# Two MLP weights decoded in a stream of their own ahead of their use, their loads on the GpSimd queue, and a later scan instruction in a complex linear attention kernel

## The chip, the cores and the metric

The kernel runs on one core of one Trainium2 chip. The time is device microseconds of one execution. Three runs of the kernel before gave 1078.79, 1084.68 and 1078.61 us, median 1078.79. Engines are named as in the profile: PE is TensorE, DVE VectorE, ACT ScalarE, POOL GpSimd, SP SyncE.

## The reference

Three stages follow each other. The attention is a linear recurrence over 768 time steps for 4 batches and 8 heads of width 48, with a complex decay per channel:

```
mag   = sqrt(a_re^2 + a_im^2);  scale = min(mag, 0.999) / (mag + 1e-6)
S_re, S_im = a_re*scale * S_re - a_im*scale * S_im + k (x) v,  a_re*scale * S_im + a_im*scale * S_re
y[t]  = q[t] . S_re
```

The 3072 tokens with their 384 channels then go through a gated MLP, `x = ((x @ w1) * (x @ w2)) @ w3 @ w_out` with a hidden width of 1024, and through a second MLP, `h = x @ w_in` of width 2048, `g = h * tanh(softplus(h))`, `out = g @ w_out2`. Everything is float32 outside the chip.

## The kernel before

**Attention.** The 768 steps of a batch are cut into chunks of 128 tokens, 24 in all. Inside a chunk the recurrence becomes matmuls on keys and queries that are scaled with running products of the decays. These products are made by `bh_stream(g)` for three groups of eight chunks; all eight chunks of a group, with both halves of each, lie side by side on 128 partitions, so that a group is 65 steps long. A group goes in blocks of 7 steps (10 blocks: nine of 7 and one of 2). For each block `norm` computes the limited decays on VectorE and ScalarE (its last results are the planes of `an`, lines 240 and 241, and the squares `rv`, line 246), `inverse` runs one scan instruction on VectorE over `rv` (line 270) for the reciprocals, `steps` does the recurrence of the products with two dependent VectorE instructions a step (lines 292 and 293), and `scaled` multiplies keys and queries by both into the tile `kt` (lines 310 and 313), which POOL's queue stores to the DRAM buffer `kq_d` with three DMAs (lines 315 and 317). `table` closes a group with six small instructions (lines 327 to 332) that need the `fs` copies of lines 299 to 302.

`ch_stream` then works chunk by chunk: it loads a chunk's keys `tm` from `kq_d` with two DMAs on SP (line 390), transposes them on TensorE (`ps_tr`, line 421), forms the chunk's contribution to the state (`ps_u`), the scores (`ps_a`, masked into `am` on VectorE) and the outputs (`ps_y`), and stores them to DRAM. Four chunks make an x tile of 512 tokens, six in all; it is loaded back as `xl` (line 496) and split into a high and a low part.

**First MLP.** Before everything else `fold_stream` multiplies w3 by w_out on TensorE. `m1_stream(i)` then takes x tile i through w1 and w2 (`pa`, `pb`) and through the folded matrix (`acc`), in eight column blocks j. Every product is three matmuls of high and low parts (`mm3`, line 549). The weights arrive as 64-bit values. `decode` loads a column block into one of two buffers `raw64` on SP's queue (line 142), and turns it into float32 with two ScalarE instructions (lines 149, 160) and two VectorE instructions (lines 161, 164); `split` then writes the high part on ScalarE (line 133) and the low part on VectorE (line 134). For w1 and w2 that is `w12(j)`, called by `m1_stream(0)` just before block j is used: 16 tiles in all, 384 KB each. The split parts take the room of the fold's buffers. The second MLP (`ps_h`, `ps_o`) follows when the first is through.

**Order.** `_merge` interleaves the streams while the program is traced: each stream yields the cost of what it just traced, and the stream with the smallest sum of cost over weight goes next. A planner then orders each engine's instructions by this order and by estimated durations; an instruction that is ready may go ahead of earlier ones that are not. On the chip each engine and each DMA queue takes its instructions in that fixed order. The merges are

```
_merge((F, 24.0), (bh_stream(0), 106.0))
_merge((until(CH, 8), 59.0), (bh_stream(1), 106.0), (take(M, 90.0), 90.0))
_merge((until(CH, 16), 59.0), (bh_stream(2), 106.0), (take(M, 90.0), 90.0))
```

with F the fold, CH the chunks and M the first MLP. Blocks of `kt` have one buffer: a block's `kt` can be written when the stores of the one before have read it.

## Time and profile before

| what | value |
|---|---|
| median of 3 runs | 1078.79 us |
| the profiled execution: span | 1079.1 us |
| PE busy | 935.3 us (87%) |
| DVE busy | 702.2 us (65%) |
| ACT busy | 691.0 us (64%) |
| POOL busy | 108.9 us (10%) |
| mean granted clock of PE | 0.944 |

The span runs from the first to the last instruction; of the profiled execution it is the only time there is. A busy share over the whole span mixes stages: the fold and the first group's scan, then chunks, scans and the first MLP side by side, then the second MLP. The rows further down are therefore taken stage by stage. A row of a timeline gives start, duration, engine, line and operation, and in brackets how long the engine was idle just before and what ended that. Instructions of one engine are pipelined, so that two which follow each other can overlap by some hundredths of a microsecond.

### The profile page before, as it was taken

What the parts mean: (1) busy time and instruction counts of PE and PEld (TensorE: products, weight loads), DVE (VectorE), ACT (ScalarE), POOL (GpSimd) and SP (SyncE); (2) the same over time, 40 slices, a digit from 0 to 9 for tenths busy, and PEclk for the clock granted to TensorE, in tenths of its full rate; (3) what the DMA queues carried; (4) which work ended last, traced back from release to release, by engine and by line L of the source; (5) the groups of instructions that cost most, each with busy time, mean ns of one, the idle gap of its engine ahead of it and who ended that gap; (6) DMA issues with size and microseconds to landing.
All of it is one profiled execution on the core that took longest, in us unless ns stands there. A gap on an engine that the chain in (4) does not pass through costs nothing.

```text
span 1079.1 us, 13826 instructions
## 1 busy us (share of the span) xinstructions
PE 935.3 (87%) x4952; PEld 754.5 (70%) x4952; DVE 702.2 (65%) x1334; ACT 691.0 (64%) x1263; POOL 108.9 (10%) x161
## 2 busy tenths in 40 slices
PE   0586006879999999999999999999999999999997
PEld 0243005758788778888888888888888888887876
DVE  5989797899898999462335522688565644645552
ACT  6987466877787686574445422998656665466672
POOL 1212242222212222000000000000000000000000
PEclk9988556889999999999999999999999999999999
DMA  8675559995786875664533300122100101000000
GB/s 304 218 242 149 155 149 249 225 248 131 199 226 163 208 219 115 160 189 115 128 64 127 87 30 29 59 89 59 59 1 10 50 1 59 1 19 10 1 30 33
DMA packets 72509, 124.36 MB, mean 115 GB/s; under 512 B 7574, under 2 KB 45776, under 8 KB 71024
## 3 DMA queue, kind: packets, MB, share of 16 engines
q1 hardware_dynamic: 60880, 85.41, 28.4%
q0 software_dynamic: 11552, 37.98, 13.5%
q8 instruction: 41, 0.67, 0.3%
q14 instruction: 36, 0.29, 0.1%
HBM read 84.16 MB, written 36.18 MB: 112 GB/s over the span
## 4 chain that ended last, share of the span: by engine, by line
PE 62%; DVE 7%; DMA 3%; ACT 2%; issue 1%; SPq 0%; DVEq 0%; ACTq 0%
PE ps_h L549 18%; PE ps_o L549 17%; PE acc L549 7%; PE pa L549 7%; PE pb L549 6%; PE ps_a L464 2%; PE ps_tr L421 2%; DMA ws<-w 1%; PE ps_u L429 1%; PE ps_y L477 1%; PE ps_y L482 1%; DVE t L292 1%; DVE kt L313 1%; DVE p L293 1%; DMA out<-osb 1%
## 5 line engine op out<-in xcount | busy, mean ns | idle before, releaser
L549 PE MATMUL ps_o<-gh,wuh 128*128 128x512 f32 x288 | 113.4, 395 | 2.0 <-ACT osb L722 1.7
L549 PE MATMUL ps_o<-gl,wuh 128*128 128x512 f32 x288 | 113.3, 393 | 0.4 <-DVE gl L134 0.4
L549 PE MATMUL ps_h<-x2h,wil 128*128 128x512 f32 x288 | 113.4, 394 | 0.0
L549 PE MATMUL ps_h<-x2h,wih 128*128 128x512 f32 x288 | 113.2, 393 | 0.0
L549 PE MATMUL ps_o<-gh,wul 128*128 128x512 f32 x288 | 112.8, 392 | 0.0
L549 PE MATMUL ps_h<-x2l,wih 128*128 128x512 f32 x288 | 112.1, 389 | 0.0
L134 DVE TENSOR_TENSOR gl<-hb,gh 128x1024 fp32r<-128x1024 f32 x48 | 58.6, 1223 | 76.2 <-ACT gh L133 76.2
L692 ACT ACTIVATE wb<-ps_h 128x512 f32<-128x512 f32 x96 | 56.1, 598 | 67.9 <-PE ps_h L549 67.7
L693 DVE COPY hb<-ps_h 128x512 f32<-128x512 f32 x96 | 64.7, 687 | 49.1 <-ACT wb L692 47.2
L571 DVE TENSOR_TENSOR u<-u,pb 128x512 f32<-128x512 f32 x48 | 32.8, 684 | 69.5 <-PE pb L549 69.3
L421 PE MATMUL ps_tr<-id_sb,tm 128*96 128x128 f32 x384 | 55.6, 288 | 25.1 <-DMA tm<-kq_d 22.5
L133 ACT CAST gh<-hb 128x1024 fp32r<-128x1024 f32 x48 | 50.2, 1048 | 35.0 <-PE ps_o L549 35.0
L421 PEld LDWEIGHTS ps_tr<-id_sb,tm 128*96 128x96 f32 x384 | 44.5, 132 | 35.5 <-issue 24.3
L292 DVE TENSOR_TENSOR t<-an,p 128x192 f32<-128x192 f32 x192 | 67.4, 351 | 0.7
L133 ACT CAST uh<-u 128x512 fp32r<-128x512 f32 x48 | 29.7, 618 | 59.6 <-DVE u L571 59.4
L180 PE MATMUL ps_f<-fw1h,fw1l 128*128 128x384 f32 x48 | 24.8, 692 | 48.7 <-DVE fw1l L164 48.7
L549 PEld LDWEIGHTS ps_o<-gh,wuh 128*128 128x128 f32 x288 | 54.0, 188 | 16.8 <-ACT osb L722 4.2
L549 PEld LDWEIGHTS ps_o<-gl,wuh 128*128 128x128 f32 x288 | 54.1, 188 | 12.7 <-DVE gl L134 1.1
L549 PEld LDWEIGHTS ps_h<-x2l,wih 128*128 128x128 f32 x288 | 54.1, 188 | 12.5
L549 PEld LDWEIGHTS ps_h<-x2h,wil 128*128 128x128 f32 x288 | 54.0, 188 | 12.5
L549 PEld LDWEIGHTS ps_o<-gh,wul 128*128 128x128 f32 x288 | 54.2, 188 | 12.0
L549 PEld LDWEIGHTS ps_h<-x2h,wih 128*128 128x128 f32 x288 | 54.1, 188 | 11.3
(177 smaller groups left out, 2402.3 us busy)
## 6 DMA issues: line engine op xcount, KB each, us to landing
tm<-kq_d SPq DMA_DIRECT2D x48, 384.0 KB, 5.9
an<-in_a POOLq DMA_DIRECT2D x27, 336.0 KB, 5.0
kqt<-in_kq POOLq DMA_DIRECT2D x27, 336.0 KB, 6.6
kq_d<-kt POOLq DMA_DIRECT2D x27, 336.0 KB, 3.9
kq_d<-kt POOLq DMA_DIRECT2D x54, 168.0 KB, 5.2
vv<-in_v SPq DMA_DIRECT2D x24, 256.0 KB, 2.8
raw<-in_w SPq DMA_DIRECT2D x16, 384.0 KB, 5.5
raw<-in_win SPq DMA_DIRECT2D x16, 384.0 KB, 4.2
```

Of the source, the lines that this page charges most:

```text
L133: A.copy(out=hi, in_=raw)
L134: V.tensor_tensor(out=lo, in0=raw, in1=hi.bitcast(F32), op=sub)
L180: T.matmul(ps, lhsT=f[:, kk], rhs=wos[:, kk], start=(kk == 0), stop=(kk == 7))
L292: V.tensor_tensor(out=t, in0=win2, in1=_bc(pv[:, ::-1], 2, 2), op=mul)
L293: V.tensor_tensor(out=p[:, j], in0=t[:, 0], in1=t[:, 1], op=add)
L313: V.tensor_tensor(out=kt, in0=_bc(kqt, 3, 2), in1=_bc(p[:, 0:m], 2, 2), op=mul)
L421: T.transpose(ps[:, hh], tm[n][:, h0 + hh, z], id_sb[0:C, 0:C])
L464: T.matmul(ps[:, hh], lhsT=kf[n][:, h], rhs=qf[n][:, h], start=True, stop=True)
L549: T.matmul(ps, lhsT=l, rhs=r, start=first and n == 0, stop=final and n == len(seq) - 1)
L571: V.tensor_tensor(out=u, in0=u, in1=pb, op=mul)
L692: A.activation(out=wb[:, f % GRP], in_=ps, func=AF.Sigmoid, scale=-1.0)
L693: V.tensor_copy(hb[:, f % 2], ps)
```

## The change

The w1 and w2 tiles get a stream of their own, `w12_stream`, merged with the second stage at weight 36. Their loads go out on POOL's queue, each ordered behind a store marked in `st["pin"]`: the last `kt` store that POOL was given up to that point of the trace. `m1_stream` draws the stream on if a block is not there yet. In `bh_stream` the scan instruction is traced after the fourth step of a block (the last one where a block is shorter) and no longer ahead of its steps. `kt` gets two buffers, and the stores of the last two blocks of group 0 go to SP's queue. To make room, `x1` takes a slot of the tag `t`, and `rz` is no longer padded to a full block.

```diff
-    def decode(src, n, dst=None, raw=None, pool=None, cap=False, signs=False):
+    def decode(src, n, dst=None, raw=None, pool=None, cap=False, signs=False, queue=None):
...
-        nc.sync.dma_start(out=raw.rearrange("p n z -> p (n z)"), in_=src.bitcast(I32))
+        (queue or nc.sync).dma_start(out=raw.rearrange("p n z -> p (n z)"), in_=src.bitcast(I32))
...
-                kt = bh.tile([128, m, 2, 2, D], F32, tag="kt", name="kt", bufs=1, padded_shape=[128, BLK, 2, 2, D])
+                kt = bh.tile([128, m, 2, 2, D], F32, tag="kt", name="kt", padded_shape=[128, BLK, 2, 2, D])
...
-                nc.gpsimd.dma_start(out=kq_d[g][0:64, s0:s0 + m], in_=kt[0:64].rearrange("p s z r d -> p s (z r d)"))
+                q = nc.sync if g == 0 and i >= NB - 2 else nc.gpsimd
+                q.dma_start(out=kq_d[g][0:64, s0:s0 + m], in_=kt[0:64].rearrange("p s z r d -> p s (z r d)"))
                 for z in range(2):
-                    nc.gpsimd.dma_start(
+                    w = q.dma_start(
...
+                if q is nc.gpsimd:
+                    st["pin"] = w
...
-            x1 = bh.tile([64, 2, 2, D], F32, tag="x1", name="x1", bufs=1)
+            x1 = bh.tile([128, 2, 2, D], F32, tag="t", name="x1")[0:64]
...
-            inverse(i)
-            yield .9
             for k, w in enumerate(steps(i)):
                 yield w
+                if k == min(3, blocks[i][1] - blocks[i][0] - 1):
+                    inverse(i)
+                    yield .9
...
-    def w12(j):
-        for src, n in ((w1, "w1"), (w2, "w2")):
-            f = decode(src[:, j], 3 * 128)
-            split(f, wt[n + "h"][:, j].rearrange("p k n -> p (k n)"), wt[n + "l"][:, j].rearrange("p k n -> p (k n)"))
+    w12_done = [0]
+
+    def w12_stream():
+        for j in range(8):
+            for src, n in ((w1, "w1"), (w2, "w2")):
+                with tc.issue_after(st["pin"].ins):
+                    f = decode(src[:, j], 3 * 128, queue=nc.gpsimd)
+                split(f, *[wt[n + z][:, j].rearrange("p k n -> p (k n)") for z in "hl"])
+            w12_done[0] = j + 1
+            yield 2.0
...
-            if i == 0:
-                w12(j)
+            while w12_done[0] <= j:
+                next(W12)
...
+    W12 = w12_stream()
     _merge((F, 24.0), (bh_stream(0), 106.0))
-    _merge((until(CH, 8), 59.0), (bh_stream(1), 106.0), (take(M, 90.0), 90.0))
+    _merge((until(CH, 8), 59.0), (bh_stream(1), 106.0), (take(M, 90.0), 90.0), (W12, 36.0))
```

## Rows read from the trace of the kernel before

**Rows 1.** Busy us by stage: PE, PEld, DVE, ACT, POOL; clock, DMA, GB/s.
```profile
171.00:226.50 55.50, 45.80 (x376) 40.60 (x376) 49.03 (x116) 46.23 (x121) 13.70 (x20) 0.80 0.95 237
277.00:300.00 23.00, 21.35 (x125) 17.29 (x124) 18.95 (x50) 18.48 (x47) 5.71 (x10) 0.93 0.80 210
...
410.00:671.00 261.00, 261.00 (x1617) 218.37 (x1616) 113.43 (x203) 120.75 (x272) 7.38 (x12) 1.00 0.39 101
```

**Rows 2.** Timeline of PE, 80 to 300 us: start, duration, idle before.
```profile
151.75 0.45 PE L401 MATMUL ps_mt<-id_sb,mt 64*96 64x64 f32 x2 [46.49 <-DVE mt L330]
171.13 2.77 PE L421 MATMUL ps_tr<-id_sb,tm 128*96 128x128 f32 x12 [18.93 <-DMA tm<-kq_d]
...
226.54 0.50 PE L549 MATMUL pa<-xh,w1h 128*128 128x512 f32 x1 [2.19 <-ACT xh L133]
```

**Rows 3.** Chain of waits, 226 to 300 us: start, us, what.
```profile
277.61 5.59 DMA raw<-in_w
```

**Rows 4.** Groups of instructions, 103 to 152 us: busy, mean ns, idle before.
```profile
L161 DVE SCALAR_TENSOR_TENSOR raw<-raw 128x384 int32<-128x384 int32 x5 | 2.8, 555 | 2.8 <-ACT raw L160 2.8
L164 DVE SCALAR_TENSOR_TENSOR dec<-dec,raw 128x384 int32<-128x384 int32 x5 | 2.8, 553 | 0.0
L149 ACT ACTIVATE dec<-raw 128x384 f32<-128x384 f32 x5 | 2.7, 545 | 10.5 <-DMA raw<-in_w 10.5
...
L134 DVE TENSOR_TENSOR w1l<-dec,w1h 128x384 fp32r<-128x384 f32 x3 | 1.7, 554 | 0.0
...
L134 DVE TENSOR_TENSOR w2l<-dec,w2h 128x384 fp32r<-128x384 f32 x2 | 1.1, 556 | 0.0
```

**Rows 5.** Timeline of DVE, 120 to 230 us.
```profile
120.75 0.96 DVE L270 TENSOR_TENSOR_SCAN rs<-rv,sc 128x384 f32<-128x384 f32 x1 [3.06 <-ACT rv L246]
...
133.81 0.56 DVE L161 SCALAR_TENSOR_TENSOR raw<-raw 128x384 int32<-128x384 int32 x1 [2.75 <-ACT raw L160]
...
144.74 0.51 DVE L238 SCALAR_TENSOR_TENSOR m<-y,m 128x336 f32<-128x336 f32 x1 [1.41 <-ACT m L234]
...
146.79 1.55 DVE L313 TENSOR_TENSOR kt<-kqt,p 128x1344 f32<-128x1344 f32 x1
...
150.99 0.20 DVE L327 TENSOR_TENSOR x<-p,fs 64x96 f32<-64x96 f32 x1
...
157.34 0.35 DVE L313 TENSOR_TENSOR kt<-kqt,p 128x192 f32<-128x192 f32 x1
...
173.65 0.35 DVE L292 TENSOR_TENSOR t<-an,p 128x192 f32<-128x192 f32 x1
...
174.74 0.36 DVE L292 TENSOR_TENSOR t<-an,p 128x192 f32<-128x192 f32 x1
...
175.43 0.36 DVE L292 TENSOR_TENSOR t<-an,p 128x192 f32<-128x192 f32 x1
```

**Rows 6.** Timeline of POOL, its stores of `kt`.
```profile
137.44 1.48 POOL L317 DMA_DIRECT2D kq_d<-kt  x2
...
148.64 0.59 POOL L315 DMA_DIRECT2D kq_d<-kt  x1 [0.30 <-DVE t L292]
...
158.56 1.08 POOL L317 DMA_DIRECT2D kq_d<-kt  x2
...
165.14 1.48 POOL L317 DMA_DIRECT2D kq_d<-kt  x2
...
194.57 1.47 POOL L317 DMA_DIRECT2D kq_d<-kt  x2
```

**Rows 7.** DMA issues, 160 to 230 us: size, median us to landing.
```profile
raw<-in_w SPq DMA_DIRECT2D x3, 384.0 KB, 6.1
```

**Rows 8.** Waits of DVE, 0 to 155 us: total, times, longest.
```profile
DVE rs L270 <- ACT rv L246: 8.1, 4, 3.1
```

**Rows 9.** Timeline of SP's queue: the keys of chunks 0 and 1.
```profile
162.14 2.86 SPq L390 DMA_DIRECT2D tm<-kq_d  x4
```

**Rows 10.** Waits of SP's queue, 145 to 175 us: total, times, longest.
```profile
SPq L142 <- DVE dec L164: 23.9, 3, 13.2
```

More of the change, by code (lines that the diff above doesn't have):

```diff
@@ L186, in fold_stream @@
             wt[n] = wpo.tile([128, 8, 3, 128], F32R, tag=n, name=n)
-    tabs = {}
+    tabs, st = {}, {}
     def bh_stream(g):
@@ L194, in bh_stream @@
         blocks = [(s0, min(s0 + BLK, L + 1)) for s0 in range(0, L + 1, BLK)]
-        ans, kqs, dec, sqs = {}, {}, {}, {}
+        ans, kqs, dec, rvs, sqs = {}, {}, {}, {}, {}
         run = {}
@@ L251, in norm @@
                 V.memset(rv[0:64, :, 1], 1.0)
-            dec[i] = (an, rv)
+            dec[i], rvs[i] = an, rv
             yield .5
@@ L258, in inverse @@
             n = s1 - s0
-            rv = dec[i][1]
+            rv = rvs.pop(i)
             add1 = sc1
@@ L266, in inverse @@
             if n < BLK:
-                add1 = bh.tile([128, D * (n + 1)], F32, tag="rz", name="rz", bufs=1, padded_shape=[128, D * (BLK + 1)]).rearrange("p (d s) -> p d s", d=D)
+                add1 = bh.tile([128, D * (n + 1)], F32, tag="rz", name="rz", bufs=1).rearrange("p (d s) -> p d s", d=D)
                 V.memset(add1, 0.0)
@@ L279, in steps @@
             n = s1 - s0
-            an, _ = dec.pop(i)
+            an = dec.pop(i)
             p = run["b"] = bh.tile([128, n, 2, D], F32, tag="p", name="p", padded_shape=[128, BLK, 2, D])
@@ L367 @@
     chunks_done = [0]
-    st = {}
     zs = [ch.tile([D2, H, DP], F32, name=f"z{z}", bufs=1) for z in range(2)]
```

## The prediction

> **What bounds the kernel now.** I read the busy time by stage first, then TensorE's timeline, then what its late starts wait for. From 410 us to the MLP's second half at 671 us TensorE is busy for all of 261 us at full clock, and the scans are no longer in its way [rows 1]. Work that is always available sets the end there, so the change can only pay by letting TensorE begin its continuous work earlier. That work begins late: after the fold TensorE sits idle for 46.5 us until the first table, then 18.9 us for the keys of chunk 0, and the first matmul on x (`pa`) starts at 226.54 us [rows 2]. Between chunk 0 and that matmul it is busy 45.8 of 55.5 us, at 0.80 of its clock [rows 1]. After it there is always an x tile or a chunk to work on, with one exception: a late w load stands in the chain of waits for 5.59 us [rows 3], and 277 to 300 us shows 21.35 busy of 23 at a clock of 0.93 [rows 1]. So the forecast is a sum over four points: the end of group 0's scan, the load of chunk 0's keys, the first `pa`, and 277 to 300 us.
>
> **Scan of group 0, the decodes leave it.** Five decodes lie beside its last third though nobody needs them yet: 5 + 5 + 3 + 2 = 15 VectorE instructions, and ScalarE waits 10.5 us for their loads [rows 4]. ScalarE works in order, so these waits reach the scan: VectorE stands 3.06, 2.75 and 1.41 us, 7.2 in sum, each time for something ScalarE writes [rows 5]. An instruction placed between two steps costs less than its 0.55 us: with a decode between them two steps start 1.09 us apart (173.65 to 174.74), without it 0.69 (174.74 to 175.43) [rows 5], so 0.40 each and 15 x 0.40 = 6.0. Removal of all is worth 13.2 us. Not all goes: the first three pairs of loads are ordered behind the third write of block 7, issued at 138.9 us before [rows 6], some 10 us earlier now; with a landing of 6.1 us [rows 7] about one tile is decoded before the scan ends, 3 x 0.40 + 7.2 / 5 = 2.6 us back. **-10.6 us**, bounds -13.2 and -5 (waits as long as before, behind other loads).
>
> **Scan instruction mid-block.** VectorE waits 8.1 us in four places for `rv` ahead of line 270 up to 155 us, 3.06 of it counted above [rows 8]; 5.0 are left. But ScalarE writes the planes that the next step multiplies (lines 240, 241) right beside `rv` (line 246), so most of this wait passes on to line 292. I take -1, bounds -5 and 0.
>
> **Keys of the last two blocks.** Block 8's `kt` is written at 146.79, its store is issued at 148.64 behind the `fs` copies, block 9's `kt` (0.35 us of work) comes only at 157.34 because the one buffer is still being read, its store ends issue at 159.64, and the load of chunk 0 is issued at 162.14 [rows 5, 6, 9]. The last step is done at 150.99 [rows 5]: 11.1 us from there to the load. Sync's queue is another holder: it waited 23.9 us in three places for raw buffers, 13.2 at the longest, ahead of that load [rows 10]; the w loads leave this queue too. After: scan, product and `kt` of block 9, about 1.0 us by their widths; three stores on sync at the 0.7 us that a key load takes there (2.86 / 4) [rows 9], 2.1; a landing of at most 162.14 - 159.64 = 2.5; together 5.6. Block 8's stores end no later: 148.3 + 2.1 + 6.1 = 156.5, against 150.99 + 5.6 = 156.6. **-5.5 us**, bounds -8 and -2. POOL loses six stores. Nothing else stands behind sync's new ones but this load, which must wait for them anyway. Chunk 0's load then goes out at 162.1 - 17.1 = 145 us; its 9.0 us to 171.13 [rows 2, 9] I leave as they are (3 either way). The second `kt` buffer costs nothing later; the shared `x1` and smaller `rz` are nothing (six instructions a group).
>
> **Chunks 0 to 3, the decodes arrive.** The order mark moves on with each POOL store of `bh_stream(1)`. By the yields (10.5 of 106 a block, 2 of 36 a pair) pairs 0 to 2 stand behind block 7 of group 0, 3 and 4 behind block 0, 5 to 7 behind blocks 1 and 2 of group 1; block 2's store was issued at 194.57 [rows 6], and now some 10 us earlier. So about ten tiles, 30 instructions, 12 us, are decoded beside chunks 0 to 3, where VectorE has 55.5 - 49.0 = 6.5 us free and ScalarE 9.3 [rows 1]; with waits for loads as above (1.4 a tile) it is 26 us. DMA engines are 0.95 busy there: ten loads of 384 KB at the 237 GB/s moved are 16.6 us against 2.8 free [rows 1]. Both are shared with the scan of group 1, which TensorE needs only at chunk 8 and which is ready in almost every gap; and the first `pa` needs only pair 0. Low end 0 (the scan yields all), high end 26 (the chunks yield all). I take a third, **+8 us**: two thirds of VectorE's time there is the scan's. The Trainium skill (DMA: Bandwidth & Descriptors, section Queues, rings and completion order) says that each DMA engine takes turns between its queues, so loads on POOL's queue would press on POOL's own transfers, not on sync's key loads; by that rule this term would be near +2, the second rival below. Nothing in these rows shows the turns. First `pa`: 226.5 - 17.1 + 8 = 217.4.
>
> **After it.** The last 6 to 7 tiles leave x tile 0. At 277 to 300 us I count the idle 1.65 us and 0.07 of 23 us, 1.6: **-3.3**, bounds -5.6 (the whole wait of the chain) and 0. From 410 us nothing changes.
>
> **Sum.** -10.6 - 1 - 5.5 + 8 - 3.3 = -12.4 us. The profiled execution has a span of 1079.1 us, 0.3 over the median of 1078.79, so nothing around the span needs adding. 1079.1 - 12.4 = 1066.7: **1067 us**, 1.1% faster. About 1%, 10.8 us, is what a measurement can tell from no change. Own range 1060 to 1073.
>
> **Rivals.** (a) **Key loads untouched**: the extra loads press only on the scan of group 1, the chunk term is 2 and the sum 18.4: 1061, 1056 to 1063. For it: sync loses 16 loads. Against: 0.95 busy engines. (b) **The decodes crowd the chunks**: VectorE and ScalarE become the bound, term 17 to 26, the first `pa` where it was, 1075 to 1084, likeliest 1078. For it: 12 us of work into 6.5 free, before any wait. Against: ten tiles have 40 us, and the scan can yield. (c) **POOL's queue holds the scan's inputs**, slower: a w load that waits for its raw buffer stands in POOL's queue ahead of `an`; sync's longest such wait was 13.2 us [rows 10]. It decides once a hold outlasts the lead of `an`, one block: blocks 0 and 2 of group 1 stored 194.57 - 165.14 = 29.4 us apart [rows 6], 14.7 each, less a landing near 6 is 8.7. Past that ScalarE waits for `an` with the chunks' copies behind it: about six holds at 13.2 - 8.7 = 4.5 us are 27 us, so 1067 + 27 = 1094. Against: the mark puts each load behind a store, and POOL is busy only 13.7 of 55.5 us [rows 1]. The Trainium skill (SBUF — State Buffer, section SBUF: two separate sides) warns that loads issued by GpSimd starve while VectorE holds a shared port; no row here shows such a stall. (d) **The load of chunk 0 moves little**: VectorE's order, planned from estimated durations, puts the last `kt` late again, or pads the room with decodes. Then only about 6 us remain: 1073 to 1076.
>
> **Chances.** Forecast 0.47, (a) 0.20, (b) 0.20, (c) 0.07, (d) 0.06. Faster by over 1% (under 1068): six tenths of the forecast's case and all of (a), 0.48. Slower by over 1% (over 1089.6): (c) and a tail of (b), 0.09. Within 1%: 0.43. The range runs from (a)'s low end to (b) without its tail, 1056 to 1082, and leaves out (c), that tail, and sums with every term at its low end, less than 2 in 10.
>
> **What would show it.** First table near 140 us, chunk 0's load near 145, `ps_tr` near 154, the first `pa` near 217, no w load in the chain at 277 to 300; no decode on VectorE between the fold's end and some 130 us. The first table earlier than 135 or later than 147 puts the first term wrong; more than 65 us from `ps_tr` to `pa` is (b), less than 58 (a); `an` loads late with ScalarE waiting for them is (c). If `pa` comes 10 us earlier and the end does not, then TensorE ran short of work between 230 and 410 us, which I have excluded.

## The result, and the profile after

The changed kernel takes 1088.74 us, median of 7 runs (1087.01 to 1091.03), against 1078.79 us of 7 runs of the kernel before on the same chip: ratio 1.0089, 95% interval 1.0062 to 1.0116. It is slower by 0.9%, where 1067 us were forecast. The profiled execution has a span of 1089.3 us, 10.2 more than before; it is the slowest of the seven (1091.03 us), 2.3 us over their median.

TensorE's timeline of the changed kernel (start, duration, idle before) at the three points of [rows 2]; the line numbers have moved by three:

```profile
138.06 0.45 PE L404 MATMUL ps_mt<-id_sb,mt 64*96 64x64 f32 x2 [25.94 <-DVE mt L333]
149.26 3.62 PE L424 MATMUL ps_tr<-id_sb,tm 128*96 128x128 f32 x16 [10.75 <-DMA tm<-kq_d]
...
238.03 0.80 PE L552 MATMUL pa<-xh,w1h 128*128 128x512 f32 x1 [2.02 <-ACT xh L133]
```

The first table is 13.7 us earlier, its distance to the first transposes of chunk 0 falls from 19.4 to 11.2 us (8.2 more), and then all of it is lost: from `ps_tr` to the first `pa` it is 88.8 us, where it was 55.4, 33.4 more. From the first `pa` to the end it is 851.3 us, where it was 852.6. -13.7 - 8.2 + 33.4 - 1.3 = +10.2. I call the time from the first `ps_tr` to the first `pa` the stretch from here on.

Busy time by stage of the changed kernel, columns as in [rows 1]; the last line is the stretch:

```profile
171.00:226.50 55.50, 42.16 (x243) 34.61 (x243) 49.18 (x115) 46.12 (x119) 15.02 (x23) 0.51 0.81 214
277.00:300.00 23.00, 22.92 (x153) 18.62 (x153) 20.42 (x62) 16.89 (x41) 7.74 (x12) 1.00 0.78 192
410.00:671.00 261.00, 261.00 (x1637) 219.20 (x1636) 107.69 (x190) 118.95 (x272) 4.77 (x8) 1.00 0.39 105
149.26:238.03 88.77, 60.49 (x356) 50.15 (x356) 73.63 (x176) 71.27 (x178) 22.32 (x35) 0.58 0.84 220
```

VectorE and ScalarE are both over four fifths busy for 89 us, and TensorE, at a clock of 0.58 of full speed, waits. From 410 us on nothing has changed. What the decodes add there, from the groups of instructions of the same stretch (busy, mean ns, idle before):

```profile
L160 ACT ACTIVATE raw<-raw,cb 128x384 int32<-128x384 uint16 x15 | 9.5, 632 | 0.0
L149 ACT ACTIVATE dec<-raw 128x384 f32<-128x384 f32 x15 | 8.2, 547 | 8.4 <-DMA raw<-in_w 8.4
L161 DVE SCALAR_TENSOR_TENSOR raw<-raw 128x384 int32<-128x384 int32 x14 | 7.5, 553 | 12.8 <-ACT raw L160 12.7
L164 DVE SCALAR_TENSOR_TENSOR dec<-dec,raw 128x384 int32<-128x384 int32 x14 | 7.4, 549 | 0.0
...
L134 DVE TENSOR_TENSOR w1l<-dec,w1h 128x384 fp32r<-128x384 f32 x7 | 3.9, 552 | 0.6 <-ACT w1h L133 0.5
L134 DVE TENSOR_TENSOR w2l<-dec,w2h 128x384 fp32r<-128x384 f32 x7 | 3.8, 550 | 0.0
L133 ACT CAST w1h<-dec 128x384 fp32r<-128x384 f32 x7 | 3.6, 508 | 0.9 <-DVE dec L164 0.9
L133 ACT CAST w2h<-dec 128x384 fp32r<-128x384 f32 x7 | 3.5, 505 | 0.0
L149 ACT ACTIVATION_READ_ACCUMULATOR dec<-raw 128x1 f32 x15 | 2.8, 187 | 0.0
```

That is 22.6 us of VectorE (7.5 + 7.4 + 3.9 + 3.8) and 27.6 us of ScalarE (9.5 + 8.2 + 2.8 + 3.6 + 3.5), on fourteen to fifteen of the sixteen tiles, and VectorE stands another 12.7 us ahead of them, each time for ScalarE, which waits 8.4 us for the loads. The work beside them has not given way. The steps of the group 1 scan in the stretch, first in the groups of the changed kernel, then in those of the kernel with the stream undone (e1 below, stretch 60.6 us):

```profile
L292 DVE TENSOR_TENSOR t<-an,p 128x192 f32<-128x192 f32 x33 | 11.4, 346 | 0.0
```

```profile
L292 DVE TENSOR_TENSOR t<-an,p 128x192 f32<-128x192 f32 x32 | 11.2, 350 | 0.0
```

The same number of steps in 89 and in 61 us: the scan keeps its place beside the chunks, and both are stretched. In the 55.4 us of the kernel before there are fewer:

```profile
L292 DVE TENSOR_TENSOR t<-an,p 128x192 f32<-128x192 f32 x25 | 8.7, 350 | 0.1
```

There ten more steps ran between the table and `ps_tr`, while TensorE stood for the keys; in the changed kernel and in e1 six do. The wait that the change shortens was not empty on VectorE, and what ran in it now falls into the stretch.

### The profile page after: what moved, and what is told of

Its sections match the earlier page's. It is cut to its first block, busy times and chain, and to the rows that moved or that the text cites. A ratio compares the mean times of both kernels' runs of the same rounds, so it can differ in the third digit from the quotient of the medians.

```text
span 1089.3 us, 13847 instructions
## 1 busy us (share of the span) xinstructions
PE 950.1 (87%) x4952; PEld 765.2 (70%) x4952; DVE 702.9 (65%) x1334; ACT 694.5 (64%) x1263; POOL 113.8 (10%) x171
## 4 chain that ended last, share of the span: by engine, by line
PE 64%; DVE 14%; ACT 9%; DMA 8%; issue 3%; POOL 0%; SPq 0%; DVEq 0%; ACTq 0%; POOLq 0%
PE ps_h L552 18%; PE ps_o L552 17%; PE acc L552 7%; PE pa L552 7%; PE pb L552 6%; PE ps_a L467 2%; DVE t L292 2%; PE ps_tr L424 2%; DMA raw<-in_w 2%; PE ps_u L432 2%; DVE p L293 2%; DVE kt L313 1%; DMA ws<-w 1%; PE ps_y L480 1%; DMA kq_d<-kt 1%
## 5 line engine op out<-in xcount | busy, mean ns | idle before, releaser
L424 PE MATMUL ps_tr<-id_sb,tm 128*96 128x128 f32 x384 | 60.6, 304 | 18.4 <-DMA tm<-kq_d 11.2
L133 ACT CAST gh<-hb 128x1024 fp32r<-128x1024 f32 x48 | 50.2, 1049 | 35.7 <-PE ps_o L552 35.7
L424 PEld LDWEIGHTS ps_tr<-id_sb,tm 128*96 128x96 f32 x384 | 47.3, 140 | 31.3 <-issue 15.1
L552 PEld LDWEIGHTS ps_o<-gl,wuh 128*128 128x128 f32 x288 | 54.1, 188 | 12.9 <-DVE gl L134 1.3
L552 PEld LDWEIGHTS ps_h<-x2l,wih 128*128 128x128 f32 x288 | 54.2, 188 | 12.5
L552 PEld LDWEIGHTS ps_h<-x2h,wil 128*128 128x128 f32 x288 | 54.1, 188 | 12.5
L180 PE MATMUL ps_f<-fw1h,fw1l 128*128 128x384 f32 x48 | 22.1, 630 | 46.6 <-DVE fw1l L164 46.6
L552 PEld LDWEIGHTS ps_o<-gh,wul 128*128 128x128 f32 x288 | 54.2, 188 | 12.0
L552 PEld LDWEIGHTS ps_h<-x2h,wih 128*128 128x128 f32 x288 | 54.1, 188 | 11.2
```

Source lines behind the costliest of these rows:

```text
L133: A.copy(out=hi, in_=raw)
L180: T.matmul(ps, lhsT=f[:, kk], rhs=wos[:, kk], start=(kk == 0), stop=(kk == 7))
L424: T.transpose(ps[:, hh], tm[n][:, h0 + hh, z], id_sb[0:C, 0:C])
L552: T.matmul(ps, lhsT=l, rhs=r, start=first and n == 0, stop=final and n == len(seq) - 1)
```

## The experiments

All of them in one table. Times are medians; the ratio is to the kernel before, run beside it on the same chip, with its 95% interval. The columns behind it are from one profiled execution, which lies up to 4.1 us beside the median of its kernel (e14; e1 3.4 below), so differences of a few us in them mean little: starts of the first `ps_mt`, `ps_tr` and `pa`; length of the stretch; VectorE's and ScalarE's busy time in it; time from the first `pa` to the end of the span. All in us.

| run | median | ratio | ps_mt | ps_tr | pa | stretch | DVE | ACT | after pa |
|---|---|---|---|---|---|---|---|---|---|
| before | 1078.79 | 1 | 151.75 | 171.13 | 226.54 | 55.4 | 49.0 | 46.2 | 852.6 |
| after | 1088.74 | 1.0089 (1.0062 to 1.0116) | 138.06 | 149.26 | 238.03 | 88.8 | 73.6 | 71.3 | 851.3 |
| e1 stream undone | 1072.27 | 0.9936 (0.9914 to 0.9959) | 145.09 | 153.72 | 214.33 | 60.6 | 55.2 | 50.2 | 852.8 |
| e2 drawn by the tile | 1091.69 | 1.0108 (1.0078 to 1.0139) | 137.32 | 146.71 | 220.94 | 74.2 | 63.8 | 58.9 | 871.0 |
| e3 no loads | 1090.51 | 1.0098 (1.0061 to 1.0135) | 138.22 | 151.18 | 240.37 | 89.2 | 74.3 | 72.0 | 848.4 |
| e4 scan at head | 1096.87 | 1.0166 (1.0129 to 1.0203) | 139.05 | 152.20 | 238.89 | 86.7 | 76.3 | 69.6 | 855.1 |
| e5 loads alone | 1072.49 | 0.9929 (0.9903 to 0.9955) | 138.96 | 157.77 | 225.48 | 67.7 | 43.0 | 41.0 | 846.3 |
| e6 matmuls, ahead | 1090.56 | 1.0113 (1.0082 to 1.0144) | 138.36 | 152.52 | 235.84 | 83.3 | 71.8 | 70.8 | 851.6 |
| e7 scan on before | 1075.47 | 0.9962 (0.9938 to 0.9985) | 144.07 | 163.02 | 222.12 | 59.1 | 52.4 | 48.8 | 850.0 |
| e8 keys on before | 1074.08 | 0.9958 (0.9940 to 0.9975) | 151.67 | 160.39 | 220.13 | 59.7 | 54.2 | 49.7 | 854.3 |
| e9 no VectorE part | 1092.48 | 1.0119 (1.0076 to 1.0161) | 137.94 | 151.25 | 239.41 | 88.2 | 59.8 | 68.3 | 850.2 |
| e10 matmuls in place | 1098.17 | 1.0148 (1.0115 to 1.0181) | 138.69 | 151.89 | 248.34 | 96.5 | 77.0 | 74.0 | 847.6 |
| e11 two pairs, SP | 1072.61 | 0.9910 (0.9878 to 0.9942) | 146.25 | 155.67 | 213.71 | 58.0 | 54.1 | 49.7 | 857.4 |
| e12 two pairs, POOL | 1082.78 | 1.0004 (0.9978 to 1.0030) | 137.81 | 151.50 | 218.32 | 66.8 | 57.1 | 52.6 | 864.7 |
| e13 no ScalarE part | 1088.73 | 1.0081 (1.0052 to 1.0110) | 137.72 | 148.43 | 237.71 | 89.3 | 76.8 | 53.9 | 847.9 |
| e14 z by VectorE | 1098.14 | 1.0151 (1.0113 to 1.0189) | 137.15 | 150.11 | 245.08 | 95.0 | 79.3 | 65.4 | 855.4 |
| e15 z by VectorE, e1 | 1077.69 | 0.9980 (0.9959 to 1.0000) | 145.67 | 155.26 | 213.66 | 58.4 | 54.2 | 40.0 | 860.9 |
| e16 two pairs, late | 1077.10 | 0.9975 (0.9953 to 0.9997) | 137.56 | 150.44 | 216.85 | 66.4 | 57.0 | 54.0 | 857.5 |
| e17 ScalarE part alone | 1086.06 | 1.0062 (1.0043 to 1.0081) | 137.75 | 151.42 | 235.34 | 83.9 | 62.6 | 69.1 | 848.0 |
| e18 VectorE part alone | 1080.11 | 1.0010 (0.9987 to 1.0033) | 138.03 | 148.57 | 230.37 | 81.8 | 76.2 | 54.6 | 847.8 |

### Where the loss sits: e1, e2

e1, the stream undone:

```diff
-            while w12_done[0] <= j:
-                next(W12)
+            if i == 0:
+                w12(j)          # as in the kernel before, loads on SP
...
-    _merge((until(CH, 8), 59.0), (bh_stream(1), 106.0), (take(M, 90.0), 90.0), (W12, 36.0))
+    _merge((until(CH, 8), 59.0), (bh_stream(1), 106.0), (take(M, 90.0), 90.0))
```

> The changed kernel with only the stream of w1/w2 undone: each pair of fragments is again loaded by SP and decoded where the first product tile reads it. The scan mid-block, the two buffers of the scaled keys and the last key writes by SP stay. Theory A (the decodes of w1/w2, standing beside the chunks with two raw buffers, cost the stretch between the first ps_tr and the first pa its 33 us more): first ps_tr within 2 us of 149, that stretch back at 55 to 60 us, first pa at 204 to 212, ps_ and table as after, the tile's old waits on raw back in 277 to 300, total 1062 to 1070. Rival T (the stretch is long because of the chunk work itself, TensorE at its lower clock level behind an earlier and emptier start): the stretch stays at 80 us or more and the total at 1084 to 1092. Rival S (the loss lies in the scan mid-block, the two buffers or SP's stores): total within 4 us of 1089 as well, with the table later than 140.

1072.27 us, 0.64% faster than before, with the other parts of the change in it; the total lies 2 us above the expected range. The stretch is 60.6 us, at the edge of what theory A said, with one to two tiles decoded in it, and `pa` is 12.2 us earlier than before (the profiled execution, 1068.87 us, is 3.4 us better than this kernel's median). T and S fall. The three starts missed: the table is at 145.09 and not 138, because w1/w2 loads on SP bring five to six decodes back ahead of it, and `ps_tr` and `pa` are 3 and 2 us later than expected. Timeline of TensorE:

```profile
145.09 0.45 PE L404 MATMUL ps_mt<-id_sb,mt 64*96 64x64 f32 x2 [33.69 <-DVE mt L333]
153.72 3.52 PE L424 MATMUL ps_tr<-id_sb,tm 128*96 128x128 f32 x16 [8.18 <-DMA tm<-kq_d]
214.33 0.72 PE L552 MATMUL pa<-xh,w1h 128*128 128x512 f32 x1
```

Its stretch, columns as in [rows 1]:

```profile
153.72:214.33 60.61, 47.41 (x376) 40.17 (x377) 55.22 (x135) 50.24 (x129) 16.89 (x25) 0.78 0.91 237
```

e2, the stream not merged, only drawn:

```diff
-    _merge((until(CH, 8), 59.0), (bh_stream(1), 106.0), (take(M, 90.0), 90.0), (W12, 36.0))
+    _merge((until(CH, 8), 59.0), (bh_stream(1), 106.0), (take(M, 90.0), 90.0))
```

> The changed kernel with the stream of w1/w2 not merged beside the chunks: it is drawn by the product tile alone, pair by pair where the tile needs it; loads stay on GpSimd's queue behind the key stores' mark. Theory A: the stretch from first ps_tr to first pa is 55 to 62 us and the total 1062 to 1074, whatever queue the loads have. Rival Q (GpSimd's queue is what costs: the loads hold up the reads of the norms and keys of the next group): the stretch shortens, but the tile's own stretch behind it lengthens by 10 us or more, total 1080 to 1092. Rival T (the clock): stretch of 80 us or more, total 1084 to 1092.

1091.69 us, a miss for A's total, and its stretch (55 to 62 us) missed as well: it is 74.2 us, 14.6 shorter than in the changed kernel with only two tiles decoded in it, but what follows `pa` is 871.0 us long, 20 more: each pair now stalls the tile that draws it. And `pa` itself starts on a weight, no longer on x:

```profile
220.94 0.80 PE L552 MATMUL pa<-xh,w1h 128*128 128x512 f32 x1 [3.27 <-ACT w1h L133]
```

With the loads on POOL and behind the mark a drawn pair is late. What Q said of the times (the loss moves behind `pa`, 1080 to 1092) holds; that POOL's queue is the reason isn't shown by this run, in which the place of the decodes changed too.

### Loads, VectorE or ScalarE: e3, e5, e9, e13, e17, e18

e3, fourteen of sixteen loads left out:

```diff
-        (queue or nc.sync).dma_start(out=raw..., in_=src.bitcast(I32))
+        if src is not None:
+            (queue or nc.sync).dma_start(out=raw..., in_=src.bitcast(I32))
...
-                    f = decode(src[:, j], 3 * 128, queue=nc.gpsimd)
+                    f = decode(src[:, j] if j == 0 else None, 3 * 128, raw=keep[n], queue=nc.gpsimd)
```

> The changed kernel with fourteen of the sixteen loads of w1/w2 left out: the first pair's words are decoded eight times over (so w1 and w2 beyond their first fragment are not used), every decode instruction and its place stay. It parts the engine time of the decodes from their waits for loads. Theory A1 (two raw buffers and loads that land later than they were planned for: the engines stand at the decodes): the waits of L149 on the DMA fall from 8 us in the stretch to under 1, the stretch shortens by 12 to 25 us from 88.8, total 1068 to 1080. Theory A2 (the decodes' own 45 us of ScalarE and VectorE work and the order of the two engines' streams): the stretch shortens by under 8 us, total 1082 to 1090.

A1 falls: the waits for loads are gone and the stretch is 89.2 us, as A2 said (the total is 0.5 us over A2's range). Groups of its stretch (L150 is L149 of the changed kernel):

```profile
L150 ACT ACTIVATE dec<-raw 128x384 f32<-128x384 f32 x14 | 7.7, 550 | 0.2 <-DMA raw<-in_win 0.2
```

The 8.4 us of waits that stand out in the changed kernel were not what held it; with them gone the engines' work takes the same time.

e5, the other half: as many bytes loaded, nothing decoded:

```diff
-                    f = decode(src[:, j], 3 * 128, queue=nc.gpsimd)
-                split(f, ...)
+                    for z in range(2):
+                        nc.gpsimd.dma_start(out=wt[n + "hl"[z]][:, j]..., in_=a[:, 4 * j:4 * j + 4]...)
```

> The changed kernel with the bytes of w1/w2 moved but not decoded: thirty-two loads on GpSimd's queue bring as many bytes of another input straight into the four weight tiles (w1 and w2 are not used), no ScalarE or VectorE instruction of the decodes is left. It is the other half of the run without loads, where the stretch stayed at 89 us. Theory A2 (the 22 us of VectorE work and 27 us of ScalarE work that the decodes add to two engines already nine tenths busy there are the loss): the stretch from first ps_tr to first pa is 54 to 64 us, first pa at 203 to 212, total 1054 to 1066. Rival D (DMA traffic or GpSimd's queue): stretch 75 us or more, total above 1075. Rival T (the lower clock in that stretch by itself): the clock stays at 0.5 to 0.67 there and the stretch at 75 us or more.

The total is 1072.49 us, 16 us less than the changed kernel, and the stretch 67.7 us; both lie between the ranges of A2 and D, and T falls with a clock of 0.83. VectorE and ScalarE are busy for only 43.0 and 41.0 us of the stretch, with 24 steps of the scan in it:

```profile
157.77:225.48 67.71, 45.21 (x397) 39.94 (x397) 43.00 (x103) 41.01 (x106) 18.21 (x29) 0.83 1.04 235
```

No raw buffer holds these loads back, and 24 of them are issued between 130 and 175 us, beside the keys of the first chunks. SP's queue in this run (the first number, the start, is what counts here; the second runs over five issues and the waits between them):

```profile
142.68 20.66 SPq L393 DMA_DIRECT2D tm<-kq_d  x5
```

and in the changed kernel:

```profile
141.31 13.85 SPq L393 DMA_DIRECT2D tm<-kq_d  x5
```

From this issue to the first `ps_tr` it is 15.1 us (157.77) against 8.0 (149.26). Of the key loads issued in these first 6 us the median takes 14.3 us from issue to landing here, and 5.5 to 9.2 in every other run. So most of the loss is the engines' work, and loads let loose cost 6 to 7 us of their own ahead of the stretch (9.4 in e3, with two loads in all). What holds this stretch at 67.7 us, with both engines under two thirds busy, was not followed up.

e9, VectorE's three instructions of each decode left out; e13, ScalarE's three:

```diff
-            V.scalar_tensor_tensor(out=low, in0=top, ...)          # e9: both out, and the split's V part
-        V.scalar_tensor_tensor(out=t, in0=t, scalar=3, in1=low, ...)
...
-        A.activation(out=f, in_=top.bitcast(F32), func=AF.Abs, ...)  # e13: both out, and the split's A part
-            A.activation(out=low, in_=raw.bitcast(U16)[:, :, 1], ...)
```

In their place GpSimd sets the low tiles (e9) or the high tiles (e13) to zero, and in e13 VectorE writes the low tiles from those zeros.

> The changed kernel with VectorE's three instructions of each of the sixteen decodes left out (47 of 0.55 us, some 22 us of them between the first ps_tr and the first pa; w1 and w2 lose their signs and low words, the low tiles are set to zero by GpSimd). ScalarE's three instructions of each, 28 us there, and all loads stay. Theory V (VectorE is the engine that sets the pace: 55 us of work in a stretch of 60 without the decodes, and its waits on ScalarE's raw fall away too): the stretch is 58 to 68 us and the total 1060 to 1073. Theory S (ScalarE's added work alone is enough, for it is as full as VectorE): the stretch stays at 76 us or more, total 1077 to 1088.

> The counterpart of the run without VectorE's part: the changed kernel with ScalarE's three instructions of each of the sixteen decodes left out and VectorE's three kept (w1 and w2 lose their exponents' form; the high tiles are set to zero by GpSimd, the low ones to zero minus zero by VectorE). Loads stay. Theory S (ScalarE sets the pace: in nearly all runs it is 78 to 86% busy in the stretch however long that is): with 28 us of its work gone the stretch is 60 to 72 us and the total 1062 to 1076. Theory O (neither engine's load but the fixed order, VectorE standing at loads and at the decodes' place, is enough by itself): the stretch stays at 82 to 90 us, total 1084 to 1092.

Neither shortens the stretch: 88.2 and 89.3 us. Theory V fell with e9. Theory S had the stretch of e9 right (its total is 4.5 us over S's range) and fell with e13, where theory O, the fixed order, came out. Busy time in the stretch of e9, then of e13:

```profile
151.25:239.41 88.16, 60.58 (x392) 51.26 (x392) 59.80 (x138) 68.32 (x180) 24.73 (x38) 0.63 0.85 227
```

```profile
148.43:237.71 89.28, 55.06 (x376) 45.84 (x377) 76.78 (x183) 53.92 (x132) 28.29 (x48) 0.65 0.90 237
```

In e9 ScalarE is busy 68.3 of 88.2 us and stands 8.7 more for loads; in e13 VectorE is busy 76.8 of 89.3 us. Either each engine holds the stretch alone, or the loads took over. e17 and e18 leave out fourteen loads as well (the diff of e3 with that of e9 or e13):

> The changed kernel with ScalarE's part of the decodes alone: VectorE's three instructions of each are left out (w1 and w2 lose signs and low words, the low tiles are zero) and fourteen of the sixteen loads too (the first pair's words are used eight times). Theory E (each of the two engines holds the stretch by itself: left without VectorE's part, ScalarE still has some 68 us to do in it, and the engine that paces is 83 to 87% occupied): stretch 78 to 84 us, total 1076 to 1084. Theory L (without VectorE's part it was the loads on two raw buffers, 8.7 us of waits and fourteen hand-backs by ScalarE, that held the stretch): 60 to 72 us, total 1060 to 1074.

> The changed kernel with VectorE's part of the decodes alone: ScalarE's three instructions of each are left out (w1 and w2 lose the form of their exponents, the high tiles are zero) and fourteen of the sixteen loads too. Theory E (VectorE has 75 us of work there whatever else is gone, and was 86% busy in the run without ScalarE's part): stretch 82 to 90 us, total 1080 to 1090. Theory L (the loads on two raw buffers hold it): 60 to 72 us, total 1060 to 1074.

Theory E holds and L falls: 83.9 us with ScalarE's part alone, 81.8 with VectorE's alone (0.2 under its range; e17's total is 2 us above its own), against 88.8 with both. What they have over a stretch with hardly any decodes depends on which. Over e1 (60.6) it is 21 to 23 us, but e1 decodes five tiles ahead of the table, which comes 7 us later there. Three runs have the table at 138, as e17 and e18 do, and few or no tiles decoded in the stretch: e5 with none (67.7), and e12 and e16 further down with two and with three to five (66.8 and 66.4). (e2, where `pa` also waits 3.3 us for a weight, has 74.2.) Over the three either part alone is worth 14 to 18 us, and both together 21 to 22. In all of them but e2, and in the changed kernel, the first `pa` starts when ScalarE has split x, not on a weight. What TensorE waits for shows how (waits in the stretch: total, times, longest), first e17, then e18:

```profile
PE ps_tr L427 <- ACT ysb L494: 12.5, 3, 5.8
```

```profile
PE ps_y L481 <- DVE w L438: 19.6, 4, 8.5
```

A chunk goes to ScalarE for its copies (`kf`, `ysb`) and to VectorE for its state and scores (`w`, `am`), in turn. In e17 its copies stand behind decodes on ScalarE, in e18 its state stands behind decodes on VectorE. Either is enough for most of what the decodes cost, which is why taking one away bought nothing while the loads stayed: 0.6 and -0.5 us, where without the loads it is 4.9 and 7.0, and removing all of the engines' work 21.

### The clock: e6, e10

e6 and e10 add eight matmuls behind each decode, e6 on finished tiles, e10 on the tile just decoded:

```diff
+                ps = mm_p.tile([128, HD], F32, tag="mm", name="ps_f")
+                for kk in range(8):
+                    T.matmul(ps, lhsT=wt[n + "l"][:, j, kk % 3], rhs=woh[:, kk], ...)   # e6: lhsT=woh[:, kk, 0:128]
```

> The changed kernel with eight 128x384 matmuls on finished tiles added behind each of the sixteen decodes (their sums are not used), so that TensorE is busier in the stretch of the chunks. Rival T (the lower clock, 0.51 in 171 to 226.5 us, lengthens the stretch): the granted clock rises to 0.75 or more and the stretch falls by 8 us or more from 88.8, total 1076 to 1082. Theory A2 (ScalarE and VectorE set the pace, the clock follows from a TensorE that waits): the clock may rise, the stretch changes by less than 5 us, total 1086 to 1096.

> The changed kernel with eight 128x384 matmuls behind each of the sixteen decodes, this time reading the tile that the decode has just filled, so that they can't run ahead of it (their sums are not used). In the run before they all ran ahead of the chunks and the clock in the stretch stayed at 0.50. Rival T (the lower clock lengthens the stretch): the clock in 170 to 210 us rises above 0.7 and the stretch falls to 80 us or less, total 1075 to 1083. Theory A2 (the clock follows): with some 25 us of matmuls more on a TensorE that waits the stretch stays within 85 to 95 us, total 1086 to 1098.

e6 doesn't answer: its matmuls depend on no decode and ran ahead of the chunks (TensorE busy 31.0 us in 100 to 150 us, 9.0 in the changed kernel), and the clock from 190 to 210 us was 0.50 as in the changed kernel. Over the stretch it was 0.64, and the stretch 83.3 us, 5.5 shorter (`ps_tr` 3.3 later, `pa` 2.2 earlier): between what T and A2 expected. In e10 the clock did rise. Its stretch:

```profile
151.89:248.34 96.45, 72.27 (x508) 63.97 (x508) 76.97 (x183) 74.04 (x191) 23.12 (x35) 0.85 0.83 216
```

The clock is 0.85 and not 0.58, and the stretch is 7.7 us longer, 1.5 over A2's range; T falls. It isn't a clean test, for the added matmuls take 33.4 us of TensorE themselves, more than the chunks' matmuls gain by the faster clock (66.3 us of instructions down to 48.3). But where the decodes are gone and nothing is added, the clock is 0.78 (e1) and 0.83 (e5): the low clock of the changed kernel comes with a TensorE that waits for the two engines. How much it adds to the stretch in its turn stays open.

### The parts that pay: e4, e7, e8

e4, the changed kernel with the scan back at the head; e7 and e8, the kernel before with the scan mid-block, and with two `kt` buffers and SP's stores:

```diff
             for k, w in enumerate(steps(i)):      # e7: added to before; e4: taken out of after
                 yield w
+                if k == min(3, blocks[i][1] - blocks[i][0] - 1):
+                    inverse(i)
+                    yield .9
```

```diff
-                kt = bh.tile(..., tag="kt", name="kt", bufs=1, ...)      # e8
+                kt = bh.tile(..., tag="kt", name="kt", ...)
+                q = nc.sync if g == 0 and i >= NB - 2 else nc.gpsimd
```

> The changed kernel with the scan put back at the head of the block, ahead of its steps; all else stays. If the scan's place is worth what the chain of group 0 showed (four waits of 3 to 8 us on ScalarE's rv), the table comes 8 to 14 us later, at 144 to 150, first ps_tr at 156 to 163, and the total is 1090 to 1100 if what follows only shifts, or 1085 to 1091 if the decodes of w1/w2 and not the keys set the first pa. If the scan mid-block is itself what costs (rival S), total 1076 to 1084.

> The kernel before with one part of the change: the scan of the running product after the fourth step of a block. By the prediction's first term it brings the table of group 0 up to 10 us earlier (151.75 us before); by the run with the scan put back, where the table came 1 us later only, it brings 1 to 2 us there. Theory (scan worth little in group 0, a few us in the later groups by fewer VectorE waits): table 149 to 152, total 1071 to 1079. Rival (scan the whole of the earlier table): table 140 to 145, total 1066 to 1072.

> The kernel before with the other part of the keys' path alone: two buffers for the scaled keys, the last two blocks' key writes of group 0 by SP. Theory (the writes of a block no longer hold the next block's scaled keys on VectorE, and the loads of the first chunk no longer wait on GpSimd's queue): table 145 to 149, first ps_tr 8 to 10 us behind it where it was 19, first pa at 212 to 218, total 1066 to 1073. Rival (these parts are worth nothing alone; the run with the stream undone got its 7 us from the scan): table 150 to 153, total 1076 to 1080.

TensorE's timeline of e7, then of e8:

```profile
144.07 0.46 PE L402 MATMUL ps_mt<-id_sb,mt 64*96 64x64 f32 x2 [33.16 <-DVE mt L330]
163.02 2.76 PE L422 MATMUL ps_tr<-id_sb,tm 128*96 128x128 f32 x12 [18.49 <-DMA tm<-kq_d]
```

```profile
151.67 0.45 PE L402 MATMUL ps_mt<-id_sb,mt 64*96 64x64 f32 x2 [44.33 <-DVE mt L331]
160.39 3.69 PE L422 MATMUL ps_tr<-id_sb,tm 128*96 128x128 f32 x16 [8.27 <-DMA tm<-kq_d]
```

Most of e4's expectations missed: the table was to come 8 to 14 us later and came 1.0 later, `ps_tr` at 152.20 and not 156 to 163; the total is in the range of a mere shift, which did not happen. The two parts act on two different distances. The scan's place brings the table 7.7 us earlier and leaves 19 us to `ps_tr`; the keys' part leaves the table and takes the 19.4 us to 8.7. In both the stretch grows by 4 us, with 29 and 31 steps of the scan in it where the kernel before has 25, so that `pa` gains only 4.4 and 6.4 us. e7 came out at the rival's table (140 to 145) and at the first theory's total. e8 came out at the rival's table (150 to 153), with the distance to `ps_tr` that the theory expected, a `pa` 2 us and a total 1 us over its ranges. In e4 the scan's place is worth 1.0 us at the table: once no decode lies ahead of the table, the scan has little left to gain there. Read the other way, from the kernel before to e4, taking the decodes out with the scan still at the head brings the table 12.7 us earlier (151.75 to 139.05; the keys' part has no share in it, by e8). The two overlap. e4 is still 8 us slower than the changed kernel, 3.8 of it in the profile behind `pa`; where was not followed up.

### Versions from these answers: e11, e12, e14, e15, e16

e11 decodes two pairs beside the chunks and draws six, each a pair ahead, with loads on SP; e12 has them on POOL; e16 is e11 with the mark moved to SP's own last stores of group 0:

```diff
-            while w12_done[0] <= j:
+            while w12_done[0] <= min(j + 1, 7):
...
-(take(M, 90.0), 90.0), (W12, 36.0))
+(take(M, 90.0), 90.0), (take(W12, 4.0), 12.0))
```

> A version meant to beat both: scan mid-block, two buffers and SP's stores stay, and of the eight pairs of w1/w2 two are decoded in a slow stream beside the first chunks, the other six are drawn by the first product tile, each one pair ahead of its use; the loads are on SP's queue, still behind the key stores' mark, so that none falls in group 0. Table at 138 to 140 as in the changed kernel, first ps_tr at 147 to 151, the stretch 62 to 67 us (four decodes: 5.5 us of VectorE work more than in the kernel with the stream undone, which has one or two), first pa at 209 to 217. Theory A2: what follows pa is 852 to 858 us long, total 1062 to 1072. Rival (the pairs drawn in the tile stall it as in the run where all eight were drawn, 19 us): total 1075 to 1085.

> The same version with the loads of w1/w2 on GpSimd's queue as in the changed kernel; it parts the queue from the place. If the queue matters (loads behind the reads of the next group's norms and the key stores), it ends 5 to 15 us later than the version on SP's queue, the loss between the first pa and 410 us; if only the place of the decodes matters, the two are within 4 us.

> The version with two pairs beside the chunks, six drawn a pair ahead, loads on SP's queue, but now behind the last key stores of group 0, which SP itself issues, so that no decode falls ahead of the table (in the run before, six fell there and the table came at 146). Table at 137 to 140, first ps_tr 9 us behind it, the stretch 62 to 68 us, first pa at 208 to 216. If the weights drawn in the tile cost no more than there (what follows pa is 857 us long), total 1062 to 1072; if the decodes that no longer fall ahead of the table stall the tile instead, it is 1075 to 1085 with first pa still early: then a decode has no cheap place before 270 us.

e11 is faster than both kernels (0.9910, interval 0.9878 to 0.9942), as e1 is (0.9936); their intervals overlap, so I can't tell which is better. Its total is 0.6 us over its range. Its table missed, 146.25: on SP's queue the mark did not keep the decodes out of group 0, five or six lie there as in e1. Where the mark does keep them out (e12, e16) the table is at 138 and most of the gain is lost again (1.0004 and 0.9975), in a stretch of 66 to 67 us and behind `pa` (857 to 865 us). e16 has the second of its expected outcomes: `pa` still early (1 us over its range), the total at 1077.10. e12 was expected to end 5 to 15 us behind e11 and ended 10 behind, but there the place of the decodes differs too, so e16 is its fair neighbour: 1077.10 against 1082.78, in intervals that touch. So what the queue alone costs is not shown.

e14 and e15 move the eight scalings of `z` to VectorE, in the changed kernel and in e1:

```diff
-            for h in range(H):
-                A.activation(out=z[:, h, 0:D], in_=w[:, h], func=AF.Copy, scale=tbs[g][:, 0, ...])
+            V.tensor_tensor(out=z[:, :, 0:D], in0=w, in1=_bc(tbs[g][:, 0, ...], 2, D), op=mul)
```

> The changed kernel with work of the chunks moved from ScalarE to VectorE: the eight scalings of z, 0.32 us each, become one VectorE multiply of 0.55 us with the table's column spread over it. Per chunk ScalarE loses 2.6 us and VectorE gains 0.55. Theory S: ScalarE's 71 us in the stretch fall to 61, the stretch to 74 to 80 us, total 1074 to 1082 by that alone, less what the later chunks gain. Theory V or O: the stretch stays at 86 us or more (VectorE has 2 us more), total 1086 to 1092.

> The same move of z to VectorE in the kernel with the stream of w1/w2 undone (1072 us), meant as a version that beats both. There VectorE is busier than ScalarE in the stretch (55.2 against 50.2 us of 60.6). Theory S: the stretch falls to 52 to 57 us and the total to 1062 to 1069. If VectorE is the bound there: stretch 60 to 63, total 1070 to 1075.

Both totals missed. ScalarE lost 5.9 us in e14's stretch, VectorE gained 5.6, and the stretch grew by 6.2: against S, as V and O had it, and with VectorE as the fuller engine (the total is 6 us over their range). e15's stretch, 58.4 us, lies between its two ranges; it keeps `pa` where e1 has it and loses 8 us behind it in the profiles, 5.4 in the medians; why is open.

## Why the prediction was wrong, step by step

**Scan of group 0 (-10.6, -1).** Right, the table at 138.06 where about 140 was forecast. The split holds in the order in which the terms were counted: the decodes gone first, 12.7 (before to e4; 13.2 forecast for all of them, and the one tile that was to come back did not: VectorE's first decode after the fold starts at 145.04), then the scan's place, 1.0 (e4 to after). In the other order it is 7.7 for the scan (e7) and 7.0 for the decodes (e1 to after, 145.09 to 138.06). Neither has a price of its own.

**Keys of the last two blocks (-5.5).** Too small. The load of chunk 0 goes out at 141.31 (145 forecast) and `ps_tr` starts at 149.26 (154). From table to `ps_tr` it is 8.2 us less; alone on the kernel before, 10.7 (e8), of which 4.3 came back in the stretch.

**Chunks 0 to 3 (+8, bounds 0 and 26).** This step failed; it measured +33.4, beyond the bound. Two things are in that number. First, the stretch was taken as 55.4 us plus the decodes. With the table at 138 and hardly a decode in it, it is 66 to 68 us (e12, e16, e5), 11 to 12 more: this was put at nothing. Part of it is the scan of group 1, whose steps had run during the wait for the keys (25 in the stretch before, 31 to 33 in e12, e16 and the changed kernel, 0.6 us each); the rest is not shown. Second, the decodes, 21 to 22 us over these runs and 28 over e1, where +8 was forecast. Here it went wrong in three places. "The scan yields": it doesn't. VectorE had 32 and 33 steps in stretches of 61 and 89 us; each engine takes its instructions in the order in which they were laid down, whatever the decodes cost. The Trainium skill says so of these two engines (PSUM — Partial Sum Buffer, section Engine vs sequencer instructions: their queues are strictly first in, first out), and the counts of steps fit it. "Ten tiles, 12 us" at 0.40 us an instruction: it was fourteen to fifteen tiles, at the full 0.55 us, 22.6 us of VectorE. And ScalarE was left out of the price: 27.6 us on an engine that had 9.3 free [rows 1]. By e17 and e18 either engine's part alone is worth 14 to 18 us over e5, e12 and e16 (21 to 23 over e1). The waits for loads, which I had taken as the upper end, are not needed for it (e3).

**The rule on the queues.** The prediction drew from the Trainium skill (DMA: Bandwidth & Descriptors, section Queues, rings and completion order) that loads on POOL's queue would not press on SP's key loads, which would put this term near +2. What the Trainium skill states there is that a DMA engine takes turns between its queues; that one queue's loads leave the other's alone was my conclusion, and e5 speaks against it: there the keys took 15.1 us from issue to use beside POOL's loads, against 8.0. In the changed kernel itself nothing of the kind stands out, for 8.0 lies within the 6.2 to 12.6 us of the other runs, and e3, with two w loads in all, has 9.4. No run shows the turns themselves.

**After it (-3.3).** 1.3 measured, less than the profiled executions scatter. 277 to 300 us gained the 1.6 us that were counted, at full clock, and no w1/w2 load is in its chain. A load of w_in stands there now (chain of waits of the changed kernel, 238 to 350 us: start, us, what), which in the kernel before was in no such chain from 226 to 350 us:

```profile
289.58 6.79 DMA raw<-in_win
```

From 310 to 350 us TensorE is busy 36.3 us where it was 38.9. So having all of w1/w2 ready early is worth hardly more than a microsecond in this profile, and its price ahead of `pa` is 17 to 24 us (`pa` at 238.03 against 220.94 in e2, 218.32 in e12, 216.85 in e16 and 214.33 in e1). In the medians the changed kernel is 16.5 us behind e1.

**Rivals.** (b) had the right mechanism, at 0.20, with the mark it was to show (over 65 us from `ps_tr` to `pa`) but a price that ended at 26 us and 1084, where 33.4 and 1088.74 were measured. (a) fell with the stretch, (d) with the load of chunk 0 at 141.31. (c) did not come: the scan of group 1 lost no steps, and ScalarE waits for no `an` in the stretch; the one such wait over 1 us from 100 to 240 us, 4.5 us, ends at 126.64, ahead of the table.

## What to carry to other kernels

Work moved off a late path is free only where the engines that take it have room; with two engines some 85% busy on a chain that goes back and forth between them, price the work on both, at its full duration, and take neither the neighbours' giving way nor one engine's slack as cover. A wait that one engine stands is not empty on the others: ask what runs in it before counting all of it as gained. When leaving out one suspect changes nothing, leave out two: here loads, VectorE's part and ScalarE's part each hid behind the others. Test the parts of a combined change one at a time: two of these three pay 0.4% each, 0.6% together, and the third costs more than both bring.

## What the runs showed of the hardware

TensorE ran at a granted clock of 0.50 to 0.58 of full speed, near its lower level of 1.2 GHz, while it waited for the two other engines, and at 0.85 when matmuls filled its waits (e10), with no gain in time. Beside loads of 192 KB on POOL's queue with nothing to hold them back, SP's first key loads of 384 KB took 14.3 us from issue to landing (e5, median), where they took 5.5 to 9.2 in the other runs. A decode of 128 x 384 elements held VectorE for three instructions of 0.55 us and ScalarE for 0.63, 0.55, 0.51 and 0.19 us.
